# Decode attention over a long K/V cache: TensorE's scores in an inner loop over the two halves of the keys, and the closing steps of a head group ahead of the next group's scores

## The chip, the cores and the metric

The kernel runs on one NeuronCore of a Trainium2 chip. The metric is the device time of one execution in microseconds. A profiled execution gives a trace of every engine: TensorE (PE, with its weight loads as PEld), VectorE (DVE), ScalarE (ACT), GpSimd (POOL) and SyncE (SP, which issues most DMAs). A letter q behind an engine's name is its sequencer, which does the waits, the branches and the register steps. The two matrix memories of the text are SBUF, where tiles lie, and PSUM, where TensorE writes its products.

## The reference

One token for each of two batch rows attends to a cache of 32,768 keys, with 32 query heads in 8 groups of 4 that share a K/V head; a small MLP makes a gate that multiplies the attention's output.

```python
xn = layernorm(x)                        # x: (2, 1, 512)
q = (xn @ wq)                            # 32 heads of 128
scores = q @ k_cache^T * 128 ** -0.5     # k_cache: (2, 8, 32768, 128) bf16, each K/V head for 4 query heads
p = softmax(scores)
s = (p @ v_cache) @ wo                   # wo: (4096, 512)
x1 = xn + hs                             # hs: a gated, time-shifted branch; with one token its shifted parts are zero
g = silu(x1 + gelu(layernorm(x1) @ w3) @ w4)
out = x + s * g
```

The two caches are 268 MB of bf16; the weights that are read are some 12 MB more.

## The kernel before

The work is cut into 16 head groups, one for each batch row and K/V head (`NG = 16`). A group's K is one SBUF tile of 8.4 MB and so is its V. `kbuf` has three half-tiles (slots) and `vbuf` two, so a group's K takes two of the three slots, in turn 0 and 1, then 1 and 2. The keys of a group are treated in two halves (`NPART = 2`), each in 8 rounds (`NR = 8`) of 16 keys on each of 128 partitions.

There is no scheduler: every engine has its own program, written out by hand, with semaphores between them. TensorE and VectorE run a loop over groups (VectorE's body holds two, `par` 0 and 1), ScalarE and GpSimd loop too, and SP's list of DMAs is written out. In a group:

- VectorE transposes K, 16 times 128x1024 int32 (L589), into four buffers `Ts` in turn. Each transpose counts up `t_vt`; from the fifth on each waits until TensorE has used the buffer (`used`).
- TensorE takes the transposes two at a time and makes the scores, four matmuls of 128x512 for each (L698), into the PSUM tile `sc[0]` for the first half and `sc[1]` for the second.
- VectorE takes each half's row maximum (`peak`, L568 and L572), TensorE spreads it (L710), VectorE makes `shift` of it (L600), ScalarE the exponentials (L491), VectorE turns these round into `pt` (L608).
- TensorE multiplies by V into `o` (L722), 32 matmuls for each half, with a `fill` matmul or two ahead of each half that only keep it busy, and then sums the exponentials over the partitions into `S` (L729). ScalarE copies `o` to `ob` (L496) once the products are done.

The **closing steps** of a group turn `o` into its slice of the attention's output. They are `head_oT` on TensorE (L660: eight small fp32 passes over `ob`), `head_on` on VectorE (L543 `den`, L546 `rec`, L547 `recm`, L552 `on`), `head_xp` on TensorE (L666) and `head_out` on VectorE (L559 `xm`, L565 `oXs`), and GpSimd's `put_o` (L513), which copies `oXs` to its place in `oX`. Before, they are done inside the next group's scores: `head_oT` between the two halves on TensorE, `head_on` after the 12th transpose on VectorE (`if i == 1 and r == 3`), `head_xp` after the 13th round on TensorE, `head_out` behind the 16th transpose. The first group does them on values that were set ahead of the loop. After the last group they are done once more, outside of the loops: TensorE goes on in `pe_output` with `head_oT`, L740, a fill, `head_xp`, and then the product with `A_wo`: L760 for five K/V heads, L750 for these summed up (`wsum`, copied by ScalarE in L646), L768 for the other three; VectorE multiplies by the gate and adds x (L647, L648), and two DMAs write the output.

SP's list of loads runs in order on one queue: the weights, K of group 0, V of group 0, then K and V of each group in turn, and last `A_wo` in six parts. Two waits hold it. K of group m waits for `pe.sem`, which TensorE counts up at the last round of the first half of group m-1 (the slot is free then); V of group m waits for `ac.sem`, which ScalarE counts up when the products with V of group m-1 are done, and so does `A_wo` for group 14's. For group 15 alone, K and V come as two DMAs each, a half at a time, with a semaphore for each half.

`t_tv` counts what TensorE has done for VectorE; in a group it counts 20 (`N_T`): the sum, the eight rounds of the first half, oT, the next rounds, xp among them, the rest, and the spread maximum. `used`, `sum_of`, `out_of` and `turned` say at which count a thing is done, and so hold the order of TensorE's program.

Of the kernel before, what the change touches and what calls it, by code (L numbers as in the profile page):

```python
# [8 lines left out]
BF16 = mybir.dt.bfloat16  # L9
# [4 lines left out]
PE = mybir.EngineType.PE  # L14
# [104 lines left out]
def kernel(  # L119
# [51 lines left out]
    def bank(name, cols=512, dt=F32):  # L171
        return psum.tile([128, cols], dt, name=name)
# [54 lines left out]
    oX = sb("oX", [128, 1 + B * Hkv, NQ], BF16)  # L227
    oXz = sb("oXz", [128, Hkv - KC, NQ, OJ - 1 + OM], BF16)

    sc = [bank(f"sc{i}") for i in range(NPART)]  # L230
    o = bank("o")
    S = bank("S")
    oT = bank("oT", rep)
# [66 lines left out]
    def order(m):  # L300
        return (1, 0) if m % 2 == 0 else (0, 1)
# [5 lines left out]
    with tc.tile_critical(sync_engine=mybir.EngineType.Pool, no_gpsimd_drain=True):  # L307
# [153 lines left out]
        for m in range(1, NG):  # L461
            base = m % 2
            if m < NG - 1:
                sp.op(lambda e, m=m, base=base: e.dma_start(
                    out=kbuf[:, base * SLOT:(base + NPART) * SLOT], in_=row_view(A_k_cache, *groups[m])),
                    (pe.sem, pe_0 + m), e_q, inc=(t_k[0], 16))
            else:
                for i, h in enumerate(order(m)):
                    sp.op(lambda e, m=m, h=h, base=base: e.dma_start(
                        out=kbuf[:, (base + h) * SLOT:(base + h + 1) * SLOT],  # L470
                        in_=row_view(A_k_cache, *groups[m])[:, h * SLOT:(h + 1) * SLOT]),
                        (pe.sem, pe_0 + m), inc=(t_k[i], 16))
            load_v(m, (ac.sem, ac_0 + m))
        for i, (a, c, r0, r1) in enumerate(wo_parts):
            cols = slice(r0 * D, r1 * D)
# [52 lines left out]
        N_T = NPART * NR + 4  # L528

        def used(par, n):  # L530
            return t_tv, par * N_T + n + 2 + (n >= NR) + (n >= NR + 5)

        def sum_of(par):
            return t_tv, par * N_T + 1

        def out_of(par, last=False):
            return t_tv, par * N_T + (2 if last else NR + 2)

        def turned(par, last=False):
            return t_tv, par * N_T + (3 if last else NR + 8)  # L540

        def head_on(c, par=0, last=False, behind=None):
            nc.vector.tensor_reduce(  # L543
                out=den[:, :], in_=S[:, 0:NPART * rep].rearrange("p (i h) -> p h i", h=rep),
                axis=AX.X, op=ALU.add).wait_op(*sum_of(par), "sem-ge").then_inc(*c.inc(t_d))
            nc.vector.reciprocal(out=rec[:, :], in_=den[:, :]).wait_op(*c.at(t_d), "sem-ge").then_inc(*c.inc(t_d))  # L546
            nc.vector.tensor_mul(  # L547
                out=recm[:, :, :], in0=rec[:, :].unsqueeze(1).broadcast_to([128, NQ, rep]),
                in1=sel_h[:, :].unsqueeze(2).broadcast_to([128, NQ, rep])).wait_op(*c.at(t_d), "sem-ge").then_inc(*c.inc(t_d))
            e = c.at(t_d)  # L550
            nc.vector.wait_ge(*out_of(par, last))
            ins = nc.vector.tensor_mul(  # L552
                out=on[:, :, :], in0=oT[:, :].unsqueeze(1).broadcast_to([128, NQ, rep]), in1=recm[:, :, :]).wait_op(*e, "sem-ge")
            if last:
                ins.then_inc(t_vt, 1)
                behind()

        def head_out(c, par=0, last=False):
            nc.vector.tensor_mul(  # L559
                out=xm[:, :, :], in0=xp_b[:, :].rearrange("p (r h) -> p r h", r=NQ),  # L560
                in1=mask[:, :].unsqueeze(1).broadcast_to([128, NQ, rep])).wait_op(*turned(par, last), "sem-ge").then_inc(*c.inc(t_d))
            with nc.allow_low_precision(reason="three of the four terms are zero, the fourth is bf16"):
                if last:
                    return ve.op(lambda v: v.tensor_reduce(out=oXz[:, Hkv - KC - 1, :, OJ * B - 1], in_=xm[:, :, :], axis=AX.X, op=ALU.add), c.at(t_d), e_xz0)
                nc.vector.tensor_reduce(out=oXs[:, :], in_=xm[:, :, :], axis=AX.X, op=ALU.add).wait_op(*c.at(t_d), "sem-ge").then_inc(t_vg, 1)  # L565
# [11 lines left out]
        with nc.body("dve_groups", valid_engines=[DVE]):  # L577
            c = Counts()
            for par in range(2):
                nc.vector.wait_ge(*c(t_z))  # L580
                for i, h in enumerate(order(par)):
                    u = par + h
                    kt = kbuf[:, u * SLOT:(u + 1) * SLOT].bitcast(I32)
                    for r in range(NR):
                        n = i * NR + r
                        events = ([c(t_k[i], 16)] if r == 0 else []) + ([used(par, n - T_BUFS)] if n >= T_BUFS else [])
                        for e in events[:-1]:
                            nc.vector.wait_ge(*e)
                        ins = nc.vector.transpose(  # L589
                            out=Ts[n % T_BUFS][:, :].rearrange("p (b t k) -> p t b k", b=NB, t=RT),  # L590
                            in_=kt[:, r * W:(r + 1) * W].rearrange("p (t b k) -> p t b k", b=NB, t=RT))
                        for e in events[-1:]:
                            ins.wait_op(*e, "sem-ge")
                        ins.then_inc(t_vt, 1)
                        if i == 1 and r == 3:
                            peak(c, 0)
                            head_on(c, par)
                head_out(c, par)
                peak(c, 1, *used(par, NT - 1))
                nc.vector.tensor_reduce(  # L600
                    out=shift[:, :], in_=S[:, NPART * rep:NPART * (rep + 32)], axis=AX.X, op=ALU.min).wait_op(t_tv, (par + 1) * N_T, "sem-ge").then_inc(t_shift, 1)
                for h in range(NPART):
                    e = c(t_e)
                    if h == NPART - 1:
                        nc.vector.tensor_mul(
                            out=sm[:, :, :], in0=sel_h[:, :].unsqueeze(1).broadcast_to([128, NPART, rep]),
                            in1=rs[:, :].unsqueeze(2).broadcast_to([128, NPART, rep])).wait_op(*e, "sem-ge").then_inc(t_vg, 1)
                    ins = nc.vector.transpose(  # L608
                        out=pt[h][:, :, :].rearrange("p r (t h) -> p t r h", h=rep),
                        in_=ep[order(par).index(h)][:, :].rearrange("p (t r h) -> p t r h", r=NR, h=rep))  # L610
                    if h < NPART - 1:
                        ins.wait_op(*e, "sem-ge")
                    ins.then_inc(t_vt, 1)
            c(t_tv, 2 * N_T)
            for s_, n in c.totals():
                take(nc.vector, s_, n)
            nc.regs_alu(turn_v, turn_v, 1, op=ALU.add)
            nc.vector.br_lt(turn_v, NG // 2, on_true="dve_groups", on_false="dve_last").branch_hint(hint_v)
        nc.switch_bb("dve_last")

        for b in range(B):
# [4 lines left out]
        e_wd, e_ws, e_s = ((pe.sem, pe.n + NG + i) for i in (1, 2, 3))  # L626


        def own_part():
# [6 lines left out]

        c = Counts()
        e_wide = (ve.sem, ve.n + 2)
        head_on(c, last=True, behind=own_part)
# [41 lines left out]
        pe.n, pe.seen = prologue.n + NG, prologue.seen  # L681
        assert prologue.n == pe_0
        turn = nc.alloc_registers("turn", engines=[PE])
        nc.regs_mov(turn, 0)
# [2 lines left out]
            nc.tensor.wait_ge(s, v)  # L687
        nc.br("pe_groups", engines=[PE])
        with nc.body("pe_groups", valid_engines=[PE]):
            for i in range(NPART):  # L690
                for r in range(NR):
                    if r % 2 == 0:
                        take(nc.tensor, t_vt, 2)
                    Tb = Ts[(i * NR + r) % T_BUFS][:, :].bitcast(BF16).rearrange("p (b c e) -> p b c e", b=NB, e=2)
                    zc = (NR - 1 - r) * rep
                    for nb in range(NB):
                        for w in range(2):
                            ins = nc.tensor.matmul(  # L698
                                sc[i][:, :], lhsT=z[:, nb, w, zc:zc + 128], rhs=Tb[:, nb, :, w],
                                start=(r == 0 and nb == 0 and w == 0),  # L700
                                stop=(r == NR - 1 and nb == NB - 1 and w == 1))
                            if i == 0 and r == NR - 1 and nb == 0 and w == 0:
                                ins.then_inc(pe.sem, 1)
                    ins.then_inc(t_tv, 1)
                    if i == 1 and r == 4:
                        head_xp()
                if i == 0:
                    head_oT()
            take(nc.tensor, t_vt)
            nc.tensor.matmul(  # L710
                S[:, NPART * rep:NPART * (rep + SREP * 32)].rearrange("p (s c) -> p s c", s=SREP), lhsT=same_h[:, :],
# [100 lines left out]
```

## Time and profile before

| | |
|---|---|
| median of 3 runs | 656.33 us (655.88, 656.33, 656.56) |
| profiled execution, first to last instruction (span) | 654.1 us |
| of the median outside of such a span | 2.2 us |
| TensorE busy | 417.4 us (64%) |
| VectorE busy | 379.4 us (58%) |
| ScalarE busy | 39.7 us (6%) |
| bytes moved by DMA | 280.54 MB, 429 GB/s over the span |

The profiled execution's own time is known by its span; the three runs were timed without it. In a line of a timeline the first number is the start in us from the span's start, the second how long the instructions took together, then engine, line, operation, tiles written and read, shapes, and how many were merged (x8); in square brackets stands how long the engine had been idle before and what ended this. In a line on sequencer steps (`PEldq`, `POOLq`) the three numbers are the shortest, the median and the longest in ns. In a line of a table by stretches stand the stretch, its length, busy time and number of instructions of each engine (PE, PEld, DVE, ACT, POOL), TensorE's granted clock as a share of full speed, the DMA engines' share and GB/s.

### The profile page before, as it was taken

To read this page: it belongs to the slowest core of one execution; us is meant where nothing else is said; L and a number is where in the kernel's file an instruction comes from. 1 tells how busy PE (TensorE), PEld (TensorE's weight loads), DVE (VectorE), ACT (ScalarE), POOL (GpSimd) and SP (SyncE) were. 2 spreads that over 40 slices of the span, in tenths; PEclk is the share of its full clock that TensorE was granted. 3 is DMA by queue.
4 is the path that set the end of the run, shared out by engine and by line. 5 is a ranking of instruction groups with operands and counts; after the bars stand their busy time and mean duration, and the time that the engine had idled before them with its cause. 6 is when DMAs were issued, how large, how long until landed. Compare 5 with 4: busy or idle time off the path is not lost. (4 is left out here: it accounts for less than half of the span.)

```text
span 654.1 us, 6304 instructions
## 1 busy us (share of the span) xinstructions
PE 417.4 (64%) x2476; PEld 159.3 (24%) x2476; DVE 379.4 (58%) x541; ACT 39.7 (6%) x90; POOL 10.3 (2%) x44
## 2 busy tenths in 40 slices
PE   1437386574858747485774838667484865748876
PEld 0013132221313212131321313222131322213223
DVE  5348193673919457291854729276481936738772
ACT  1200101000010100001000010100001010000101
POOL 1000000000000000000000000000000000000000
PEclk9859889697997969899796989969698896979999
DMA  8999999999999999998999999999999899999997
GB/s 367 435 449 449 442 393 449 445 449 401 437 445 449 433 405 449 445 449 389 449 445 449 417 421 445 449 445 393 449 445 449 389 449 445 449 425 411 437 429 292
DMA packets 6246, 280.54 MB, mean 429 GB/s; under 512 B 730, under 2 KB 868, under 8 KB 1380
## 3 DMA queue, kind: packets, MB, share of 16 engines
q1 hardware_dynamic: 6232, 280.50, 99.2%
q8 instruction: 2, 0.03, 0.0%
q10 hardware_dynamic: 12, 0.00, 0.0%
HBM read 280.50 MB, written 0.00 MB: 429 GB/s over the span
## 5 line engine op out<-in xcount | busy, mean ns | idle before, releaser
L589 DVE STREAM_TRANSPOSE T<-kbuf 128x1024 int32<-128x1024 int32 x256 | 294.8, 1211 | 180.1 <-DMA kbuf<-in_A_k_cache_dram 173.2
L698 PE MATMUL sc<-T,z 128*128 128x512 bf16 x1024 | 273.1, 420 | 179.5 <-PEq L482 179.2
L698 PEld LDWEIGHTS sc<-T,z 128*128 128x128 bf16 x1024 | 98.9, 104 | 346.6 <-issue 260.2
L722 PE MATMUL o<-vbuf,pt 128*16 128x512 bf16 x1024 | 70.4, 379 | 17.7 <-PEq L482 17.7
L491 ACT ACTIVATE ep<-sc,shift 128x512 bf16<-128x512 f32 x32 | 21.7, 683 | 502.7 <-ACTq L482 502.7
L722 PEld LDWEIGHTS o<-vbuf,pt 128*16 128x16 bf16 x1024 | 27.3, 88 | 64.9 <-issue 42.8
L568 DVE TENSOR_REDUCE mx<-sc 128x1 f32<-128x512 f32 x32 | 21.5, 672 | 30.1 <-PE sc L698 30.1
L673 PE MATMUL pro<-ob,comb 128*2 128x512 f32 x66 | 33.7, 592 | 0.0
L608 DVE STREAM_TRANSPOSE pt<-ep 128x512 bf16<-128x512 bf16 x32 | 22.6, 708 | 15.0 <-ACT ep L491 15.0
L710 PE MATMUL S<-mxr,same_h 128*128 128x448 f32 x32 | 15.8, 576 | 18.4 <-PEq L482 18.4
L660 PEld LDWEIGHTS oT<-sel_o,ob 128*128 128x128 f32 x136 | 17.7, 191 | 3.4 <-issue 0.7
L729 PE MATMUL S<-sm,ones_f 128*128 128x448 f32 x32 | 16.3, 592 | 0.0
L660 PE MATMUL oT<-sel_o,ob 128*128 128x4 f32 x136 | 16.2, 242 | 0.0
L600 DVE TENSOR_REDUCE shift<-S 128x1 f32<-128x64 f32 x16 | 3.6, 225 | 18.8 <-PE S L710 18.8
L496 ACT COPY ob<-o 128x512 f32<-128x512 f32 x16 | 9.4, 587 | 78.6 <-ACTq L482 78.6
L513 POOL COPY oX<-oXs 128x4 bf16 (+1 forms) x16 | 3.0, 188 | 518.7 <-POOLq L482 518.7
L710 PEld LDWEIGHTS S<-mxr,same_h 128*128 128x128 f32 x32 | 4.8, 188 | 26.1 <-issue 26.1
L572 DVE TENSOR_SCALAR mxr<-row_of,mx 128x32 f32<-128x32 f32 x32 | 7.7, 241 | 1.1
L673 PEld LDWEIGHTS pro<-ob,comb 128*2 128x2 f32 x66 | 4.2, 83 | 14.0 <-issue 10.4
L393 PE MATMUL qrb<-ident,xs_bf 34*128 34x34 bf16 x4 | 0.3, 198 | 11.1 <-DVE xs_bf L356 11.1
L729 PEld LDWEIGHTS S<-sm,ones_f 128*128 128x128 f32 x32 | 4.8, 188 | 6.9 <-issue 6.9
L506 POOL TENSOR_TENSOR z<-qr,quad 128x64 bf16<-128x64 bf16 x16 | 4.7, 294 | 103.2 <-POOLq L482 87.7
(100 smaller groups left out, 78.5 us busy)
## 6 DMA issues: line engine op xcount, KB each, us to landing
kbuf<-in_A_k_cache_dram SPq DMA_DIRECT2D x2, 4096.0 KB, 22.4
vbuf<-in_A_v_cache_dram SPq DMA_DIRECT2D x2, 4096.0 KB, 21.7
kbuf<-in_A_wq_dram SPq DMA_DIRECT2D x1, 4096.0 KB, 12.4
vbuf<-in_B_w_dram SPq DMA_DIRECT2D x2, 1792.0 KB, 18.0
kbuf<-in_A_wo_dram SPq DMA_DIRECT2D x1, 2048.0 KB, 30.8
kbuf<-in_A_wo_dram SPq DMA_DIRECT2D x3, 512.0 KB, 31.9
kbuf<-in_A_wo_dram SPq DMA_DIRECT2D x1, 384.0 KB
kbuf<-in_A_k_cache_dram SPq DMA_DIRECT2D x15, 27.5
```

The lines of the kernel that those rows point to most:

```text
L491: nc.scalar.activation(out=ep[i][:, :], in_=sc[i][:, :], func=ACT.Exp, scale=inv_sqrt_dh, bias=shift[:, :], accum_out=rs[:, i:i + 1]).then ...
L496: nc.scalar.copy(out=ob[:, :], in_=o[:, :]).then_inc(t_ob, 1)
L568: ins = nc.vector.tensor_reduce(out=mx[:, i:i + 1], in_=sc[i][:, :], axis=AX.X, op=ALU.max)
L572: ins = nc.vector.tensor_scalar_mul(out=mxr[:, i, :], in0=row_of[:, :], scalar1=mx[:, i:i + 1]).wait_op(*c.at(t_d), "sem-ge")
L589: ins = nc.vector.transpose(out=Ts[n % T_BUFS][:, :].rearrange("p (b t k) -> p t b k", b=NB, t=RT), in_=kt[:, r * W:(r + 1) * W].rearrange ...
L608: ins = nc.vector.transpose(out=pt[h][:, :, :].rearrange("p r (t h) -> p t r h", h=rep), in_=ep[order(par).index(h)][:, :].rearrange("p (t ...
L660: ins = nc.tensor.matmul(oT[:, :], lhsT=ob[:, t * Dh:(t + 1) * Dh], rhs=sel_o[:, t, :], start=(t == 0), stop=(t == VT - 1))
L673: nc.tensor.matmul(pro[0:B, :], lhsT=comb[:, 0:B], rhs=ob[:, :], start=True, stop=True)
L698: ins = nc.tensor.matmul(sc[i][:, :], lhsT=z[:, nb, w, zc:zc + 128], rhs=Tb[:, nb, :, w], start=(r == 0 and nb == 0 and w == 0), stop=(r = ...
L710: nc.tensor.matmul(S[:, NPART * rep:NPART * (rep + SREP * 32)].rearrange("p (s c) -> p s c", s=SREP), lhsT=same_h[:, :], rhs=mxr[:, :, :]. ...
L722: ins = nc.tensor.matmul(o[32 * j:32 * j + VT * rep, :], lhsT=pt[h][:, r, a * VT * rep:(a + 1) * VT * rep], rhs=vt[:, u * VT:(u + 1) * VT, ...
L729: nc.tensor.matmul(S[:, 0:SSUM * NPART * rep].rearrange("p (s c) -> p s c", s=SSUM), lhsT=ones_f[:, :], rhs=sm[:, :, :].rearrange("p i h - ...
```

## The change

TensorE's body of a group now begins with `head_oT`, a wait for VectorE's `on`, and `head_xp`; only then come the scores. These are a loop of the machine over the two halves (`nc.Fori`), whose body holds 8 rounds, 32 matmuls; before, all 16 rounds were written out. The two score tiles become one tile of two banks, `sc2`, and the matmuls write to a column that comes from the loop's register. TensorE counts up `pe.sem` in each half, so twice a group, and the waits of K's loads are renumbered to the same event as before.

VectorE's body of a group now begins with `head_on`, the wait for GpSimd's `z`, and `head_out`; then come all 16 transposes, with the first half's maximum behind the 12th as before. `on` counts up `t_vt`, for TensorE to wait on. The counts in `used`, `out_of` and `turned` follow. The end of the kernel keeps its order.

```diff
@@ buffers
-    sc = [bank(f"sc{i}") for i in range(NPART)]
+    sc2 = bank("sc", 512 * NPART)
+    sc = [sc2[:, 512 * i:512 * (i + 1)] for i in range(NPART)]
@@ the loads of K
-                    (pe.sem, pe_0 + m), e_q, inc=(t_k[0], 16))
+                    (pe.sem, pe_0 + NPART * (m - 1) + 1), e_q, inc=(t_k[0], 16))
...
@@ counts
         def used(par, n):
-            return t_tv, par * N_T + n + 2 + (n >= NR) + (n >= NR + 5)
+            return t_tv, par * N_T + n + 4
...
-        def out_of(par, last=False):
-            return t_tv, par * N_T + (2 if last else NR + 2)
-
-        def turned(par, last=False):
-            return t_tv, par * N_T + (3 if last else NR + 8)
+        def out_of(par):
+            return t_tv, par * N_T + 2
+
+        def turned(par):
+            return t_tv, par * N_T + 3
...
@@ head_on
-            if last:
-                ins.then_inc(t_vt, 1)
+            ins.then_inc(t_vt, 1)
+            if behind:
                 behind()
...
@@ VectorE's body of a group
             for par in range(2):
+                head_on(c, par)
                 nc.vector.wait_ge(*c(t_z))
+                head_out(c, par)
                 for i, h in enumerate(order(par)):
...
                         if i == 1 and r == 3:
                             peak(c, 0)
-                            head_on(c, par)
-                head_out(c, par)
                 peak(c, 1, *used(par, NT - 1))
...
@@ TensorE's body of a group
-            for i in range(NPART):
+            head_oT()
+            take(nc.tensor, t_vt)
+            head_xp()
+            with nc.Fori(0, NPART, engines=[PE]) as i:
                 for r in range(NR):
                     if r % 2 == 0:
                         take(nc.tensor, t_vt, 2)
-                    Tb = Ts[(i * NR + r) % T_BUFS][:, :].bitcast(BF16).rearrange("p (b c e) -> p b c e", b=NB, e=2)
+                    Tb = Ts[r % T_BUFS][:, :].bitcast(BF16).rearrange("p (b c e) -> p b c e", b=NB, e=2)
...
-                                sc[i][:, :], lhsT=z[:, nb, w, zc:zc + 128], rhs=Tb[:, nb, :, w],
+                                sc2[:, bass.ds(i * 512, 512)], lhsT=z[:, nb, w, zc:zc + 128], rhs=Tb[:, nb, :, w],
...
-                            if i == 0 and r == NR - 1 and nb == 0 and w == 0:
+                            if r == NR - 1 and nb == 0 and w == 0:
                                 ins.then_inc(pe.sem, 1)
                     ins.then_inc(t_tv, 1)
-                    if i == 1 and r == 4:
-                        head_xp()
-                if i == 0:
-                    head_oT()
```

More of the change, by code (lines that the diff above doesn't have):

```diff
@@ L471 @@
                         in_=row_view(A_k_cache, *groups[m])[:, h * SLOT:(h + 1) * SLOT]),
-                        (pe.sem, pe_0 + m), inc=(t_k[i], 16))
+                        (pe.sem, pe_0 + NPART * (m - 1) + 1), inc=(t_k[i], 16))
             load_v(m, (ac.sem, ac_0 + m))
@@ L530, in used, with head_on @@
         def used(par, n):
-            return t_tv, par * N_T + n + 2 + (n >= NR) + (n >= NR + 5)
+            return t_tv, par * N_T + n + 4
         def sum_of(par):
             return t_tv, par * N_T + 1
-        def out_of(par, last=False):
-            return t_tv, par * N_T + (2 if last else NR + 2)
-        def turned(par, last=False):
-            return t_tv, par * N_T + (3 if last else NR + 8)
-        def head_on(c, par=0, last=False, behind=None):
+        def out_of(par):
+            return t_tv, par * N_T + 2
+        def turned(par):
+            return t_tv, par * N_T + 3
+        def head_on(c, par=0, behind=None):
             nc.vector.tensor_reduce(
@@ L550, in head_on @@
             e = c.at(t_d)
-            nc.vector.wait_ge(*out_of(par, last))
+            nc.vector.wait_ge(*out_of(par))
             ins = nc.vector.tensor_mul(
                 out=on[:, :, :], in0=oT[:, :].unsqueeze(1).broadcast_to([128, NQ, rep]), in1=recm[:, :, :]).wait_op(*e, "sem-ge")
-            if last:
-                ins.then_inc(t_vt, 1)
+            ins.then_inc(t_vt, 1)
+            if behind:
                 behind()
@@ L560, in head_out @@
                 out=xm[:, :, :], in0=xp_b[:, :].rearrange("p (r h) -> p r h", r=NQ),
-                in1=mask[:, :].unsqueeze(1).broadcast_to([128, NQ, rep])).wait_op(*turned(par, last), "sem-ge").then_inc(*c.inc(t_d))
+                in1=mask[:, :].unsqueeze(1).broadcast_to([128, NQ, rep])).wait_op(*turned(par), "sem-ge").then_inc(*c.inc(t_d))
             with nc.allow_low_precision(reason="three of the four terms are zero, the fourth is bf16"):
@@ L625 @@
                 in1=sel_h[:, :].unsqueeze(1).unsqueeze(3).broadcast_to([128, KW, rep, NQ])), e_oX[m + KW - 1])
-        e_wd, e_ws, e_s = ((pe.sem, pe.n + NG + i) for i in (1, 2, 3))
+        e_wd, e_ws, e_s = ((pe.sem, pe.n + NPART * NG + i) for i in (1, 2, 3))
         def own_part():
@@ L638 @@
         e_wide = (ve.sem, ve.n + 2)
-        head_on(c, last=True, behind=own_part)
+        head_on(c, behind=own_part)
         e_oX[NG - 1] = head_out(c, last=True)
@@ L680 @@
         prologue, pe = pe, Queue(nc.tensor, pe.sem)
-        pe.n, pe.seen = prologue.n + NG, prologue.seen
+        pe.n, pe.seen = prologue.n + NPART * NG, prologue.seen
         assert prologue.n == pe_0
```

## The prediction

> **What bounds the kernel now.** I read the page first: its span and its DMA queue.
>
> ```profile
> span 654.1 us, 6304 instructions
> q1 hardware_dynamic: 6232, 280.50, 99.2%
> ```
>
> One queue carries all 280.50 MB, and its packets fill 99.2% of the span. So the kernel is a stream of K and V loads with everything else laid beside it, and a change to the compute can matter in two ways only: if it makes a load start too late to keep the queue full, or if it makes the work behind the last loads end later than they land. For the first I read the timeline of a group in the middle (SPq rows are DMA issues, L448 a V load, L464 a K load).
>
> ```profile
> 304.54 1.02 PE L729 MATMUL S<-sm,ones_f 128*128 128x448 f32 x2
> 304.78 0.33 SPq L448 DMA_DIRECT2D vbuf<-in_A_v_cache_dram  x1
> 312.62 5.75 DVE L589 STREAM_TRANSPOSE T<-kbuf 128x1024 int32<-128x1024 int32 x5 [11.89 <-DMA kbuf<-in_A_k_cache_dram]
> 324.21 0.33 SPq L464 DMA_DIRECT2D kbuf<-in_A_k_cache_dram  x1
> ```
>
> VectorE waited 11.89 us for K. The V load behind that K was issued at 304.78, 7.8 us before the K landed, so the queue never ran dry. The closing sum of the group before (L729) began at 304.54: VectorE and TensorE have 8.08 us in which nothing else can start, because the next group's K is not there. For the second way I read the chain of waits and the last groups.
>
> ```profile
> 617.12 33.53 DMA kbuf<-in_A_wo_dram
> ```
>
> The chain that ended last is the load of `A_wo`, the last load of all; L768, L647 and L648 follow it. Here is how groups 14 and 15 lie before it.
>
> ```profile
> 583.11 5.75 DVE L589 STREAM_TRANSPOSE T<-kbuf 128x1024 int32<-128x1024 int32 x5 [10.97 <-DMA kbuf<-in_A_k_cache_dram]
> ...
> 598.10 0.16 DVE L543 TENSOR_REDUCE den<-S 128x4 f32<-128x8 f32 x1
> ...
> 598.80 4.61 DVE L589 STREAM_TRANSPOSE T<-kbuf 128x1024 int32<-128x1024 int32 x4
> ...
> 612.08 9.13 DVE L589 STREAM_TRANSPOSE T<-kbuf 128x1024 int32<-128x1024 int32 x8 [1.76 <-DMA kbuf<-in_A_k_cache_dram]
> ...
> 614.12 1.02 PE L729 MATMUL S<-sm,ones_f 128*128 128x448 f32 x2
> ...
> 621.88 4.62 DVE L589 STREAM_TRANSPOSE T<-kbuf 128x1024 int32<-128x1024 int32 x4 [0.67 <-DMA kbuf<-in_A_k_cache_dram]
> ...
> 627.97 4.61 DVE L589 STREAM_TRANSPOSE T<-kbuf 128x1024 int32<-128x1024 int32 x4
> ...
> 643.29 1.02 PE L729 MATMUL S<-sm,ones_f 128*128 128x448 f32 x2
> ```
>
> Group 15 is unlike the others: its K comes in two halves, and the first is there at 612.08, before group 14 is done on TensorE (L729 at 614.12). Today VectorE starts on it at once. This is the one place where the kernel uses the overlap that the change gives up.
>
> **The closing steps in the middle groups: nothing.** Their chain is head_oT (TensorE), `on` (VectorE), head_xp (TensorE), `xm` and `oXs` (VectorE). The kernel runs the same chain at its end, where nothing hides it:
>
> ```profile
> 644.31 1.02 PE L660 MATMUL oT<-sel_o,ob 128*128 128x4 f32 x8
> 645.45 0.17 DVE L552 TENSOR_TENSOR on<-oT,recm 128x16 bf16<-128x16 f32 x1 [0.52 <-PE oT L660]
> 646.30 0.18 PE L666 MATMUL xp<-on,sel_w 128*128 128x16 bf16 x1
> 646.52 0.17 DVE L559 TENSOR_TENSOR xm<-xp,mask 128x16 f32<-128x16 f32 x1 [0.28 <-PE xp L666]
> 646.73 0.18 DVE L564 TENSOR_REDUCE oXz<-xm 128x4 bf16<-128x16 f32 x1
> ```
>
> From the start of L729 at 643.29: oT starts 1.02 later, and `on` ends at 645.62, 2.33 after. At the end of the kernel head_xp stands behind other work; without it TensorE would take up `on` as it takes up `mxr` in the next two rows, 0.14 after its end (606.53 to 606.67).
>
> ```profile
> 606.29 0.24 DVE L572 TENSOR_SCALAR mxr<-row_of,mx 128x32 f32<-128x32 f32 x1
> 606.67 0.99 PE L710 MATMUL S<-mxr,same_h 128*128 128x448 f32 x2 [1.15 <-PEq L482]
> ```
>
> Then 0.22 from xp to `xm` and 0.21 to the reduction, whose successor on VectorE starts about 0.1 later: 2.33 + 0.14 + 0.22 + 0.21 + 0.1 = 3.0 us from L729 to the first transpose that VectorE may now do. In a middle group K lands 8.08 after L729, so 5.1 us are to spare, and the closing chain costs nothing there. What queues behind the new waits is, on VectorE, all 16 transposes of the next group, and on TensorE its scores; on SP, the next K load waits for the first half's last round (the new count names the same event: one increment for each half, and NPART*(m-1)+1 is the first of group m-1), so its issue stays where it is. GpSimd's put_o follows `oXs` and comes earlier; put_z keeps its place.
>
> **Inside a group: 0.70 us saved.** `den`, `rec`, `recm` and `on` stood between the 12th and the 13th transpose, from 598.10 to 598.80. They go, and the rest of the group moves up by 0.70. `xm` and `oXs` stood where VectorE waits for TensorE's last scores anyway: nothing. In the middle groups the 0.70 only lengthens the wait for K. oT (0.95 us on TensorE) leaves the boundary between the halves, where VectorE sets the pace: nothing.
>
> **The inner loop.** It adds a backward branch between the halves, and an output address from a register. The nearest rows are the outer loop's branch on TensorE and the register step that GpSimd makes for an address that depends on its loop:
>
> ```profile
> L734 PEldq COMPARE_BRANCH  x16: 76/208/228, 70.6 to 641.8; - x16
> L506 POOLq FUSED_REGOPS  x15: 55/55/55, 67.7 to 609.8; - x15
> ```
>
> The branch is 0.21 us. It takes the place of 0.95 us of oT, on an engine that waits for transposes in the second half. For the register step the ends are: nothing (one step for a pass, or steps beside running matmuls), and 0.055 us on each of 32 matmuls, unhidden. A gain is excluded, because VectorE paces the half. I take nothing: matmuls are queued ahead of the array, and 0.055 fits into the 0.245 of each (the row under the rivals). The upper end is a rival below.
>
> **Group 15: where the time comes from.** All of this goes by the profiled execution. Group 14 starts at 583.11 as before, since K sets it, and is 0.70 shorter: L729 at 613.42. VectorE starts group 15 at 613.42 + 3.0 = 616.42, 4.34 later than the 612.08 of today. Both halves of K are there by 621.88, and the 9th transpose, eight spacings of 1.14 (13.74 for 12, below) after 616.42, comes at 625.5, so it waits for no K. How long it then takes to the 13th transpose is read from whole groups: 583.11 to 598.80 is 15.69 in group 14, and the longest and the shortest of groups 0 to 14 are these two:
>
> ```profile
> 158.14 5.75 DVE L589 STREAM_TRANSPOSE T<-kbuf 128x1024 int32<-128x1024 int32 x5 [11.47 <-DMA kbuf<-in_A_k_cache_dram]
> ...
> 174.43 1.24 DVE L589 STREAM_TRANSPOSE T<-kbuf 128x1024 int32<-128x1024 int32 x1
> 274.01 13.74 DVE L589 STREAM_TRANSPOSE T<-kbuf 128x1024 int32<-128x1024 int32 x12 [11.55 <-DMA kbuf<-in_A_k_cache_dram]
> ...
> 289.22 2.36 DVE L589 STREAM_TRANSPOSE T<-kbuf 128x1024 int32<-128x1024 int32 x2
> ```
>
> That is 16.29 and 15.21. What differs is how long TensorE's clock stays at half. I take group 14's 15.69, less 0.70: 14.99. The 13th transpose then starts at 616.42 + 14.99 = 631.41, against 627.97: 3.44 later. From there to L729 it is 15.32 in both groups (598.80 to 614.12, 627.97 to 643.29), so nothing in that stretch waits for a load, and L729 comes at 643.29 + 3.44 = 646.73.
>
> The clock bears on this. In the middle groups it is at half when scores start:
>
> ```profile
> 310.00:312.00 2.00, 0.00 (x0) 0.00 (x0) 0.00 (x0) 0.00 (x0) 0.00 (x0) 0.50 1.14 492
> ```
>
> This is 4.4 to 6.4 us after TensorE's last work (305.56). [...]
>
> **How much the end can hide.** These rows are the stretch behind L729 at the end.
>
> ```profile
> 646.41 1.04 PE L760 MATMUL qrb<-kbuf,T 128*2 128x512 bf16 x16
> 647.29 0.39 PE L760 MATMUL qrb<-kbuf,oX 128*2 128x512 bf16 x4
> 648.62 0.61 PE L768 MATMUL pro<-kbuf,oXz 128*4 128x128 bf16 x16 [0.94 <-DMA kbuf<-in_A_wo_dram]
> 649.07 0.81 PE L750 MATMUL pro<-T,comb 128*4 128x128 f32 x8
> 649.74 0.43 PEld L768 LDWEIGHTS pro<-kbuf,oXz 128*4 128x4 bf16 x16 [0.15 <-DMA kbuf<-in_A_wo_dram]
> 650.69 0.62 PE L768 MATMUL pro<-kbuf,oXz 128*4 128x128 bf16 x16 [0.33 <-DMA kbuf<-in_A_wo_dram]
> 647.74 0.59 ACT L646 COPY T<-qrb 128x512 f32<-128x512 f32 x1 [3.57 <-PE qrb L760]
> 651.35 0.28 DVE L647 TENSOR_TENSOR sg<-pro,g 36x128 f32<-36x128 f32 x1 [4.29 <-PE pro L768]
> ```
>
> Now 8.06 us from L729 (643.29) to `sg` (651.35), with waits for A_wo inside. Without them: L760 runs on to 647.29 (its second group starts before the first has ended, so no wait); the copy of `wsum` ends at 648.33, and L768's first 16 fit beside it; L750 at about 648.43, the next 16 of L768 0.65 later at 649.08 (649.07 to 649.74, less the wait), the last 16 another 0.43 on at 649.51, and `sg` 0.66 after that (650.69 to 651.35): 650.17. This is 6.88 us, so 1.2 us of the delay is hidden by the load. `sg` comes at 646.73 + 6.88 = 653.61, against 651.35: 2.26 later.
>
> **Sum.** 3.44 - 1.18 = 2.3 us, with 1.8 and 2.9 at the two ends of the row of groups. The span is 654.1; the runs shown are 655.88, 656.33 and 656.56, 2.2 above it at the median. The delay is added to that: 656.33 + 2.3 = 658.6, own range 657.7 to 659.6 with 0.3 for the spread of runs.
>
> **The rivals.** First, TensorE becomes the pace in the scores. At full clock 8 score matmuls take
>
> ```profile
> 632.73 1.96 PE L698 MATMUL sc<-T,z 128*128 128x512 bf16 x8 [0.26 <-PEq L482]
> ```
>
> 0.245 each. With 0.055 unhidden on each, four take 1.20, over the 1.145 of a transpose (13.74 for 12 above): 0.055 in each of 16 rounds, and 0.44 in the last two rounds that VectorE waits for, 1.3 us a group. It counts in groups 14 and 15 alone: 2.6 us more, 661.2. It decides from 0.04 us a matmul on. For it: no row shows TensorE with a register address. Against it: GpSimd's step is taken once for an instruction, and here 32 share one address. 0.13.
>
> Second, not slower: the load of A_wo still ends last and hides all. That holds while group 15 is late by under 1.2 us, and gives 656.3 to 656.9. For it: today's chain ends in that load. Against it: the 13th transpose would have to come 12.7 us after 616.42, and 12 transposes alone take 13.74; only loads that land 2 us later relative to group 14's K would do it, and the three runs lie within 0.7. 0.10.
>
> Third, the queue runs dry: if the loop added more than the 5.1 us to spare in each group, every microsecond over it would be paid in 15 groups, 671 for one. Nothing in the rows comes near: 0.03. That it gets faster has no row for it, as the queue is full: 0.02.
>
> **How the numbers follow.** The forecast has 0.72. About 0.2% (1.3 us) is what a measurement here can tell from no change. Same: the second rival and 0.04 from the forecast's low edge, 0.14. Slower: the rest of the forecast, the first and third rivals, 0.84. The range takes the forecast's own and reaches to the first rival above and half way to the second below: 656.9 to 661.4.
>
> **What would show it.** In the changed profile: the middle groups' transposes still wait for K; the closing chain lies 1 to 3 us behind L729; the 13th transpose comes 15.0 after the first; group 15's first transpose starts 3.0 behind L729 of group 14, not on a K landing; the last L768 shows no wait for A_wo, and the chain that ended last runs back through L729 and the transposes of group 15. It is wrong if that chain still ends in the A_wo load, if score matmuls are spaced over 0.285, or if issues on SP come after the K before them has landed.

## The result and the profile after

The change takes 658.87 us (657.43 to 659.56 in 8 runs), against 656.29 before, also in 8 runs. One of the 8 before took 1381.36 us, for a reason that nothing here shows, and is left out of the ratio; the other seven lie between 655.88 and 656.56. The ratio is 1.0038, with a 95% interval from 1.0029 to 1.0048: slower by 2.6 us, where 2.3 was forecast. The profiled execution spans 656.8 us, 2.7 more than that of before. Line numbers move by a few after the edit: K's transposes are L592, the scores L702, `den` L544, `oXs` L566, oT L661, xp L667, `sg` L648; L729, L760 and L768 keep theirs.

The page's head and queue, and the waits of VectorE (engine, line, for whom, us in total, times, longest):

```profile
span 656.8 us, 6464 instructions
q1 hardware_dynamic: 6232, 280.50, 98.8%
DVE den L544 <- PE S L729: 77.4, 16, 4.9
DVE T L592 <- DMA kbuf<-in_A_k_cache_dram: 74.6, 15, 6.5
```

Before, the second of these waits was:

```profile
DVE T L589 <- DMA kbuf<-in_A_k_cache_dram: 173.2, 17, 12.7
```

VectorE's wait for K fell from 173.2 us in 17 waits to 74.6 in 15, and 77.4 us of wait for the group before came in. Read by itself this looks like a large shift; it is one idle stretch cut in two by the closing steps, which now lie inside it. The queue still fills 98.8% of the span. The chain of waits has changed its kind. These are steps of it, from the last closing sum to the gate:

```profile
647.52 0.95 PE S L729 x2
...
650.63 1.18 PE qrb L760 x20
...
653.11 0.91 PE pro L768 x32
...
654.05 0.29 DVE sg L648
```

No load is in the chain any more; before, 33.5 us of it were the load of `A_wo`. Groups 14 and 15 in the timeline:

```profile
578.48 0.17 DVE L566 TENSOR_REDUCE oXs<-xm 128x4 bf16<-128x16 f32 x1
583.47 5.83 DVE L592 STREAM_TRANSPOSE T<-kbuf 128x1024 int32<-128x1024 int32 x5 [4.83 <-DMA kbuf<-in_A_k_cache_dram]
586.14 9.23 PE L702 MATMUL sc<-T,z 128*128 128x512 bf16 x32 [7.91 <-PEq L483]
...
597.70 0.65 DVE L569 TENSOR_REDUCE mx<-sc 128x1 f32<-128x512 f32 x1
598.53 4.62 DVE L592 STREAM_TRANSPOSE T<-kbuf 128x1024 int32<-128x1024 int32 x4
...
613.86 1.02 PE L729 MATMUL S<-sm,ones_f 128*128 128x448 f32 x2
...
616.75 0.17 DVE L566 TENSOR_REDUCE oXs<-xm 128x4 bf16<-128x16 f32 x1
616.84 5.82 DVE L592 STREAM_TRANSPOSE T<-kbuf 128x1024 int32<-128x1024 int32 x5
...
632.12 4.62 DVE L592 STREAM_TRANSPOSE T<-kbuf 128x1024 int32<-128x1024 int32 x4
634.63 1.96 PE L702 MATMUL sc<-T,z 128*128 128x512 bf16 x8 [1.16 <-PEq L483]
...
647.45 1.02 PE L729 MATMUL S<-sm,ones_f 128*128 128x448 f32 x2
```

And two rows of group 14 in the kernel before, its first scores and the maximum of its first half:

```profile
585.62 9.32 PE L698 MATMUL sc<-T,z 128*128 128x512 bf16 x32 [8.66 <-PEq L482]
...
597.26 0.65 DVE L568 TENSOR_REDUCE mx<-sc 128x1 f32<-128x512 f32 x1
```

Group 14 still waits 4.83 us for K after its closing steps are done. Group 15 starts at 616.84, straight behind `oXs` and with no wait in brackets: its K had been there. In the kernel before, it started at 612.08. The 4.76 us of delay become 4.15 at the 13th transpose (632.12 against 627.97) and 4.16 at L729, since the 12 transposes and the maximum took 15.28 where before group 15 took 15.89 with `head_on` and a wait for K's second half inside. Part of the 4.16 costs nothing, since the kernel before waits behind L729 for the load of `A_wo`. The same stretch in the change:

```profile
650.56 1.04 PE L760 MATMUL qrb<-kbuf,T 128*2 128x512 bf16 x16
651.43 0.39 PE L760 MATMUL qrb<-kbuf,oX 128*2 128x512 bf16 x4
651.64 0.61 PE L768 MATMUL pro<-kbuf,oXz 128*4 128x128 bf16 x16
...
652.51 0.61 PE L750 MATMUL pro<-T,comb 128*4 128x128 f32 x8
652.94 1.06 PE L768 MATMUL pro<-kbuf,oXz 128*4 128x128 bf16 x32
```

From 647.45 to `sg` at 654.05 are 6.60 us, with no wait for `A_wo`; before they were 8.06 with such waits. So 1.46 us are hidden, and 4.16 - 1.46 = 2.70 is what `sg` comes later (654.05 against 651.35), the whole of the difference between the two spans. Of the 2.70, 0.36 came in ahead of both groups: K of group 14 landed that much later in this execution (583.47 against 583.11).

### The profile page after: what moved, and what is told of

Same layout as the page of the kernel before. It is cut to its first block, busy times and chain, and to the rows that moved or that the text cites. A ratio compares the mean times of both kernels' runs of the same rounds, so it can differ in the third digit from the quotient of the medians.

```text
span 656.8 us, 6464 instructions
## 1 busy us (share of the span) xinstructions
PE 435.1 (66%) x2476; PEld 162.9 (25%) x2476; DVE 384.3 (59%) x541; ACT 39.7 (6%) x90; POOL 10.3 (2%) x44
## 3 DMA queue, kind: packets, MB, share of 16 engines
q1 hardware_dynamic: 6232, 280.50, 98.8%
## 5 line engine op out<-in xcount | busy, mean ns | idle before, releaser
L702 PE MATMUL sc<-T,z 128*128 128x512 bf16 x1024 | 278.5, 426 | 155.4 <-PEq L483 153.1
L592 DVE STREAM_TRANSPOSE T<-kbuf 128x1024 int32<-128x1024 int32 x256 | 296.6, 1215 | 84.7 <-DMA kbuf<-in_A_k_cache_dram 74.6
L702 PEld LDWEIGHTS sc<-T,z 128*128 128x128 bf16 x1024 | 99.8, 104 | 327.5 <-issue 240.8
L544 DVE TENSOR_REDUCE den<-S 128x4 f32<-128x8 f32 x17 | 2.8, 165 | 77.4 <-PE S L729 77.4
L661 PEld LDWEIGHTS oT<-sel_o,ob 128*128 128x128 f32 x136 | 17.3, 199 | 15.6 <-issue 15.6
L661 PE MATMUL oT<-sel_o,ob 128*128 128x4 f32 x136 | 18.3, 258 | 3.6 <-PEq L483 3.6
L729 PE MATMUL S<-sm,ones_f 128*128 128x448 f32 x32 | 16.3, 592 | 0.0
L553 DVE TENSOR_TENSOR on<-oT,recm 128x16 bf16<-128x16 f32 x17 | 3.0, 175 | 10.0 <-PE oT L661 10.0
L440 PE MATMUL sc<-vbuf,h_bf 128*2 128x512 bf16 x14 | 6.1, 624 | 2.4 <-DVE h_bf L437 2.4
```

What stands on the lines that cost most here:

```text
L592: ins = nc.vector.transpose(out=Ts[n % T_BUFS][:, :].rearrange("p (b t k) -> p t b k", b=NB, t=RT), in_=kt[:, r * W:(r + 1) * W].rearrange ...
L661: ins = nc.tensor.matmul(oT[:, :], lhsT=ob[:, t * Dh:(t + 1) * Dh], rhs=sel_o[:, t, :], start=(t == 0), stop=(t == VT - 1))
L702: ins = nc.tensor.matmul(sc2[:, bass.ds(i * 512, 512)], lhsT=z[:, nb, w, zc:zc + 128], rhs=Tb[:, nb, :, w], start=(r == 0 and nb == 0 and ...
L729: nc.tensor.matmul(S[:, 0:SSUM * NPART * rep].rearrange("p (s c) -> p s c", s=SSUM), lhsT=ones_f[:, :], rhs=sm[:, :, :].rearrange("p i h - ...
```

## The experiments

Theory A is that of the prediction: VectorE starts group 15 late, and nothing else costs. Theory B is that the inner loop costs, by its branch or by the column from a register. Each time stands beside that of the kernel before on the same chip, and each ratio is to that.

### The two parts of the change alone

**Closing steps ahead, scores written out.**

```diff
-            with nc.Fori(0, NPART, engines=[PE]) as i:
+            for i in range(NPART):
...
-                                sc2[:, bass.ds(i * 512, 512)], lhsT=z[:, nb, w, zc:zc + 128], rhs=Tb[:, nb, :, w],
+                                sc[i][:, :], lhsT=z[:, nb, w, zc:zc + 128], rhs=Tb[:, nb, :, w],
```

> The closing steps ahead of the scores as in the change, but all 16 rounds of scores written out, with no inner loop and no column from a register. Theory A (the cost is the late start of group 15 alone, and the inner loop costs nothing): 658.6 to 659.0 us, as the change; first transpose of group 15 3.0 us behind the closing sum of group 14; the step from the first to the second half's scores falls from 0.82 to about 0.25 us and nothing else gets shorter by it. Rival B (the inner loop's branch and register column are what costs): 656.3 us, as before.

**Inner loop, closing steps inside the scores** (here against the change; the counts in `used` and `turned` follow). TensorE does oT ahead of its loop and xp behind it, so the order is not quite that of the kernel before; what matters is that VectorE may again start a group as soon as K lands.

```diff
@@ VectorE's body of a group
-                head_on(c, par)
                 nc.vector.wait_ge(*c(t_z))
-                head_out(c, par)
...
                             peak(c, 0)
+                            head_on(c, par)
                 peak(c, 1, *used(par, NT - 1))
+                head_out(c, par)
@@ TensorE's body of a group
             head_oT()
-            take(nc.tensor, t_vt)
-            head_xp()
             with nc.Fori(0, NPART, engines=[PE]) as i:
...
+            head_xp()
             take(nc.tensor, t_vt)
```

> The inner loop over the halves as in the change, but the closing steps back inside the scores: head_oT ahead of TensorE's loop, head_on behind VectorE's 12th transpose, head_xp behind TensorE's loop, head_out behind the second half's maximum. VectorE can again start group 15 when its first half of K lands. Theory A: 656.3 us within 0.5, as before, the load of A_wo ends the kernel again. Rival B: 658.9 us, as the change.

**The change again.**

> The change itself, on the same chip as the others of this call: 658.9 us by both theories. Its profile gives a second look at the same sum: group 15's first transpose 3.0 us behind the closing sum of group 14, 15.33 us from the 13th transpose to the last closing sum, and 15.0 to 15.8 between first and 13th transpose, by the phase of TensorE's clock.

Measured, against 656.10 us before on this chip: without the loop 658.16 us, ratio 1.0036 (1.0022 to 1.0049); with the loop and the closing steps inside 655.98, ratio 0.9999 (0.9990 to 1.0008); the change 659.00, ratio 1.0038 (1.0024 to 1.0052). The first two runs say the same from two sides: the order is what costs, and the loop by itself costs nothing that shows. Without the loop 658.16 lies below the 658.6 that A had named, while its interval covers the change's ratio; whether the loop adds some tenths of a microsecond once the order has put it on the path of the end, the times don't settle, but two profiles further down do. In the timeline of the run with the loop and the old order, group 15 starts when its K lands, and the last line is from its chain of waits:

```profile
612.37 4.62 DVE L590 STREAM_TRANSPOSE T<-kbuf 128x1024 int32<-128x1024 int32 x4 [1.68 <-DMA kbuf<-in_A_k_cache_dram]
```

```profile
617.48 33.45 DMA kbuf<-in_A_wo_dram
```

`A_wo` ends the kernel again. What the loop itself adds is seen in the sequencer steps of the change (ns: shortest, median, longest):

```profile
L702 PEldq FUSED_REGOPS  x32: 46/46/46, 43.4 to 629.3; - x32
L694 PEldq COMPARE_BRANCH  x32: 76/144/225, 51.0 to 637.0; - x32
```

There are 32 register steps, one for each half of each of 16 groups, not one for each of 1024 matmuls. Eight score matmuls still take 1.96 us (634.63 above). Only the start moves: in the run without the loop the first score comes 2.50 us after the first transpose (the first two of the next rows), in the change 2.67 (583.47 to 586.14) and 2.51 before (583.11 to 585.62). The x40 says that the scores of the two halves run on there without a break.

```profile
617.13 5.74 DVE L592 STREAM_TRANSPOSE T<-kbuf 128x1024 int32<-128x1024 int32 x5
619.63 12.05 PE L702 MATMUL sc<-T,z 128*128 128x512 bf16 x40 [2.84 <-PEq L483]
...
632.59 1.24 DVE L592 STREAM_TRANSPOSE T<-kbuf 128x1024 int32<-128x1024 int32 x1
```

The second profile of the change, from the same chip, has these rows:

```profile
617.11 5.82 DVE L592 STREAM_TRANSPOSE T<-kbuf 128x1024 int32<-128x1024 int32 x5
...
632.74 2.36 DVE L592 STREAM_TRANSPOSE T<-kbuf 128x1024 int32<-128x1024 int32 x2
```

In these two profiles TensorE's clock is back at full speed in the same half microsecond (591.0 to 591.5 in group 14, 625.0 to 625.5 in group 15), so they can be compared. From the first to the 13th transpose of group 15 it is 15.46 us without the loop and 15.63 with it, and 15.47 (583.35 to 598.82) and 15.64 (583.16 to 598.80) in group 14. So in this pair the loop costs 0.17 us in each of the two groups, 0.3 us of the change's 2.6 to 2.9. In the run with the loop and the old order the chain ends in the load of `A_wo`, and the time is no longer than before.

### When group 15 starts

If the start of group 15 sets the end, a later start must cost more, whatever the order. Both kernels were run with the K of the last group as one DMA.

```diff
-        nc.gpsimd.sem_inc(t_k[1], 16 * (NG - 1))
+        nc.gpsimd.sem_inc(t_k[1], 16 * NG)
...
             base = m % 2
-            if m < NG - 1:
+            if m < NG:
```

> The kernel before, with K of the last group as one DMA in place of two halves, so that group 15 cannot start on TensorE's or VectorE's side before all of its K has landed (621.9 in the trace of before). Theory A (the end is set by when VectorE starts group 15): first transpose at 621.9, 13th 15.7 later at 637.6, 9.6 later than before, of which the load of A_wo hides 1.2 to 1.5: 656.3 + 8.2 = 664.5 us. Rival C (the last loads set the end, and compute at the end has room): 656.3 to 657.

> The change, with K of the last group as one DMA. Now the closing steps have their room in group 15 too, since the K lands 5 us behind them. Theory A: the same start as the run with the kernel before, less the 0.70 us that head_on takes inside the group: 663.8 us, and so faster than that run by 0.5 to 0.9. Rival B (the loop or the order costs time of its own): slower than that run by 2 to 3 us.

Measured, against 655.93 before: the kernel before with K whole 663.87 us, ratio 1.0123 (1.0108 to 1.0139); the change with K whole 663.84, ratio 1.0118 (1.0103 to 1.0134). The first is 0.6 below the 664.5 that A had named. Rival C is out: the loads are the same bytes in the same order, and the end moved by 7.9 us. Rival B, which asked for 2 to 3 us, is out: with the same start the change is not slower. The starts are in the timelines, first the kernel before, then the change:

```profile
621.72 5.75 DVE L589 STREAM_TRANSPOSE T<-kbuf 128x1024 int32<-128x1024 int32 x5 [11.09 <-DMA kbuf<-in_A_k_cache_dram]
627.85 8.00 DVE L589 STREAM_TRANSPOSE T<-kbuf 128x1024 int32<-128x1024 int32 x7 [0.38 <-PE sc L698]
635.78 0.65 DVE L568 TENSOR_REDUCE mx<-sc 128x1 f32<-128x512 f32 x1
...
637.32 4.61 DVE L589 STREAM_TRANSPOSE T<-kbuf 128x1024 int32<-128x1024 int32 x4
```

```profile
621.75 5.83 DVE L592 STREAM_TRANSPOSE T<-kbuf 128x1024 int32<-128x1024 int32 x5 [5.34 <-DMA kbuf<-in_A_k_cache_dram]
628.04 1.25 DVE L592 STREAM_TRANSPOSE T<-kbuf 128x1024 int32<-128x1024 int32 x1 [0.46 <-PE sc L702]
629.75 6.88 DVE L592 STREAM_TRANSPOSE T<-kbuf 128x1024 int32<-128x1024 int32 x6 [0.46 <-PE sc L702]
636.55 0.65 DVE L569 TENSOR_REDUCE mx<-sc 128x1 f32<-128x512 f32 x1
...
637.39 4.62 DVE L592 STREAM_TRANSPOSE T<-kbuf 128x1024 int32<-128x1024 int32 x4
```

Three starts of group 15 (612.1, 616.8 and 621.7) go with 656, 658.9 and 663.9 us. From the second to the third, where nothing is hidden any more, 4.9 us of start make 5.0 us of time.

What A had expected between these two runs, 0.5 to 0.9 us in favour of the change, did not show. The rows say where it went in this pair. `head_on` is gone: from the maximum to the 13th transpose it is 0.84 us against 1.54, the 0.70 saved. But the first 12 transposes took 14.80 against 14.06, as VectorE waited twice for TensorE and not once. Two things lie behind this in the traces. By stretches of half a microsecond the granted clock is at half until about 627.9 in the kernel before and until about 629.9 in the change; and with the loop the sixth transpose comes 6.29 us after the first, not 6.13. With four runs each, a gain of a few tenths in the time is neither shown nor excluded.

### TensorE's clock at the start of group 15

```diff
             head_xp()
+            fill(6)
             with nc.Fori(0, NPART, engines=[PE]) as i:
```

> The change with six fill matmuls (about 0.5 us each) behind head_xp, which keep TensorE busy until the scores of group 15 start; in the middle groups some 4 us without work remain. Theory A with its clock term: TensorE is at full speed when group 15's scores start, VectorE waits for no buffer, the 13th transpose comes 14.5 us after the first where the change has 15.28, and the time falls by 0.7 to 0.9 us on average, to 658.0 to 658.2, with less spread among runs. Rival (the clock at the start does not matter, VectorE sets the pace): 15.3 and 658.9 us.

Measured: 658.71 us against 656.10 before, ratio 1.0044 (1.0030 to 1.0058), no gain. The edit was mis-sized, and the timeline shows it:

```profile
615.95 5.31 PE L674 MATMUL pro<-ob,comb 128*2 128x512 f32 x12
621.20 4.02 PE L703 MATMUL sc<-T,z 128*128 128x512 bf16 x17
```

Six fills are 12 passes and 5.31 us, and the scores had to wait for them. So it was run with three.

> The change with three fills behind head_xp. The run with six showed that a fill takes 0.88 us, not 0.5, so that six held TensorE's scores of group 15 back by 2.2 us. Three end at about 618.6, just before the scores of group 15 can start. Theory A with its clock term: full speed from the first score of group 15, no wait of VectorE for a buffer, 14.4 us from the first to the 13th transpose (15.3 and 15.6 in the two profiles of the change), 658.0 to 658.3 us. Rival (the clock does not matter): 658.9.

Measured: 658.07 us (657.19 to 658.65 in 7 runs), ratio 1.0029 (1.0018 to 1.0040), against 655.96 before. Two stretches of a table by stretches (the granted clock stands ahead of the last two numbers), the first from the change, the second from this run, and then this run's timeline:

```profile
620.00:622.00 2.00, 2.00 (x6) 0.62 (x5) 2.00 (x3) 0.00 (x0) 0.00 (x0) 0.50 1.22 524
```

```profile
620.00:622.00 2.00, 1.45 (x7) 0.69 (x8) 2.00 (x3) 0.00 (x0) 0.00 (x0) 1.00 0.91 393
```

```profile
617.66 13.62 DVE L592 STREAM_TRANSPOSE T<-kbuf 128x1024 int32<-128x1024 int32 x12
...
632.05 1.24 DVE L592 STREAM_TRANSPOSE T<-kbuf 128x1024 int32<-128x1024 int32 x1
```

At full clock (1.00 in all four stretches from 616 to 624) the 12 transposes run through without a wait, and it is 14.39 us from the first to the 13th, as expected, where the change, at 0.50 in the stretch above, has 15.28. That the clock sets this stretch is shown in the trace. A gain in time is not: against the kernel before on its own chip this run is 2.1 us slower, where the change was 2.6 and 2.9, and the intervals overlap. In its profiled execution, the longest of the seven, K of group 14 landed at 584.09, 0.62 later than in that of the change, so group 15 started 0.82 later (617.66), its 13th transpose came 0.07 earlier, and both spans are 656.8.

### How much the load of A_wo hides

A delay of known length was put on the closing chain of the kernel before, on VectorE behind `on` (two and six memsets). Line numbers move by two in these runs: L762 is the L760 of before, L770 the L768.

```diff
         def own_part():
+            for j in range(6):
+                nc.vector.memset(kbuf.bitcast(F32)[:, SLOT // 2 + 512 * j:SLOT // 2 + 512 * (j + 1)], 0.0)
```

> The kernel before, with two memsets of 128x512 f32 (0.54 us each) on VectorE behind `on` of the last closing, ahead of the product that TensorE's first matmuls with A_wo wait for: 1.1 us on the closing chain at the end. Theory A (the load of A_wo hides 1.2 by the prediction, 1.46 by the trace of the change): 656.3 us, no change. Rival (nothing hides there): 657.4.

> The kernel before, with six such memsets in the same place: 3.24 us on the closing chain at the end. Theory A: 3.24 less 1.2 to 1.46, so 658.1 to 658.3 us, and the chain that ended last no longer ends in the load of A_wo. Rival (nothing hides there): 659.5.

Measured: with two 655.99 us, ratio 1.0001 (0.9992 to 1.0010), against 655.93 before. The profile has them at 1.03 us, and `sg` where it was (651.34 against 651.35):

```profile
645.67 1.03 DVE L631 MEMSET kbuf<- 128x512 f32 x2
...
651.34 0.28 DVE L649 TENSOR_TENSOR sg<-pro,g 36x128 f32<-36x128 f32 x1 [3.64 <-PE pro L770]
```

So at least 1.0 us is hidden. With six: 659.38, ratio 1.0049 (1.0035 to 1.0063): 3.4 us, all of the delay and more, as the rival had it. Here the timeline of the end:

```profile
645.47 3.19 DVE L631 MEMSET kbuf<- 128x512 f32 x6
649.35 1.88 PE L762 MATMUL qrb<-kbuf,T 128*2 128x512 bf16 x16 [3.09 <-DVE T L636]
654.90 0.28 DVE L649 TENSOR_TENSOR sg<-pro,g 36x128 f32<-36x128 f32 x1 [5.24 <-PE pro L770]
```

The 16 matmuls behind the memsets took 1.88 us and not 1.04: TensorE had been idle for 3.09 us and ran at half its clock (the granted clock is 0.50 from 647.5 to 654.0). So the rival's number came out by another way, and one more run had to tell them apart, with three more fills ahead of head_xp at the end (`fill(4)` for `fill(1)`), so that TensorE stays busy beside the memsets.

> The run with six memsets on the closing chain at the end, and four fills in place of one ahead of head_xp there, so that TensorE is not left idle for 3.1 us behind the memsets. In the run without them its first matmuls with A_wo took 1.88 us for 16, twice the 1.04 of before, so its 3.4 us contain a slower clock. Theory A (the load of A_wo hides 1.46): the memsets delay by 3.03, so 656.0 + 3.03 - 1.46 = 657.6 us, and those 16 take 1.04 again. Rival (nothing hides, the memsets cost their full length): 659.0 to 659.4.

Measured: 657.58 us, ratio 1.0025 (1.0015 to 1.0035), against 655.96 before.

```profile
643.08 1.02 PE L731 MATMUL S<-sm,ones_f 128*128 128x448 f32 x2
649.35 1.04 PE L762 MATMUL qrb<-kbuf,T 128*2 128x512 bf16 x16 [0.51 <-DVE T L636]
652.83 0.28 DVE L649 TENSOR_TENSOR sg<-pro,g 36x128 f32<-36x128 f32 x1 [3.18 <-PE pro L770]
```

With the 16 back at 1.04, the run costs 1.6 us. How much is hidden follows from the rows: from the last closing sum to `sg` it is now 9.75 us (643.08 to 652.83), against 6.60 in the change, where nothing waits for `A_wo`, and 8.06 in the kernel before. So the memsets delay by 3.15 us, a little more than the 3.03 that was expected, and cost 1.69: 1.46 us are hidden, as in the change's own trace.

No version came out that beats both kernels. The one with the loop and the closing steps inside equals the kernel before, and there the queue is full and the last load ends the work.

## Why the prediction was right

The mechanism and the sign were as forecast, and the size nearly: 658.87 against 658.6, well inside 656.9 to 661.4. By its steps, in the profiled execution:

- **Middle groups, nothing.** Right. `oXs` is done at 578.65, K lands 4.83 us later by the wait; 5.1 were said to be to spare.
- **3.0 us from L729 to the first transpose.** 2.98 (613.86 to 616.84).
- **0.70 saved inside a group.** 0.71 from the maximum to the 13th transpose (597.70 to 598.53, against 597.26 to 598.80 before). But not all of it reached the 13th transpose, by the next point: that came 15.06 after the first, where 15.69 less 0.70 is 14.99.
- **The inner loop, nothing.** Not quite. The rival with a register step on each matmul is out, as there is one for a half. What the prediction did not price is the start: the first score comes 0.16 later. While the clock is at half, VectorE waits for the buffers that these scores release (0.46 us ahead of the sixth transpose of group 15, at 623.12), so this is passed on: 0.17 us a group in the pair of profiles above, in the two groups that count.
- **14.99 us from the first to the 13th transpose of group 15.** 15.28, inside the ends of its row of groups (16.29 and 15.21, less 0.70). In the second profile of the change it was 15.63 (617.11 to 632.74), a little over the upper of these, 15.59.
- **15.32 from there to L729.** 15.33.
- **6.88 from L729 to `sg`.** 6.60: the hidden part was put at 1.2 and is 1.46. Of the 0.28, 0.22 is one step, from L750 to the second 16 of L768: the prediction took 0.65, though its own rows less their wait give 0.52 (0.67 - 0.15), and it is 0.43 (652.51 to 652.94).

The misses of 0.29 in group 15 and of 0.28 at the end have opposite signs and nearly cancel, which is luck. What is left between the 2.26 of the sum and the 2.70 of the profile is K of group 14, which landed 0.36 later than in the profile of before, and 0.08 from group 14 itself. The landing is no part of the sum, and whether the change has a part in it is open: it came at 583.16 in the second profile of the change.

The rival "the load hides all" was right in its mechanism: it does hide 1.0 us in full, as the two memsets show, and by the 1.46 it would have decided if group 15 had been late by less than that.

## What to carry to other kernels

A kernel whose DMA queue is 99% full can still be slowed by a reordering (2.6 us here), and the place to look is the last pass, where, as here, no wait for a load is left between two groups: ask there what started early before and what it now waits for, and take off what the last load still hides. In the middle of such a kernel large shifts in the waits (here 77 us from one cause to another) may cost nothing. A step that is free while something hides it, such as the loop here, has its price once another change puts it on the path (0.17 us in each of two groups). A delay put on one engine as a probe can change another's clock (six memsets on VectorE left TensorE at 0.50), so keep that engine busy while probing.

## What the runs showed of the hardware that I had not expected

A pause of 3.09 us on TensorE in the run with six memsets was enough to halve its clock for the work behind it (16 matmuls in 1.88 us and not 1.04). By stretches of half a microsecond, the granted clock fell at about 647.2, 0.9 us after TensorE's last matmul (xp, done at 646.26), and was back at about 654.0. In the kernel before, it fell 2.6 us after the last matmul of group 13 (576.96 to 579.52) and 4.3 us after that of group 6 (305.56 to 309.87), and it stayed at 1.00 through a gap of 1.86 us in group 14 (up to 601.31). So the length of a gap alone does not tell; what sets the moment of the fall, no run here shows. The stretches at half clock, worked out from the same half microseconds, come in few lengths: about 3.4 us ahead of group 14's scores with six fills (586.3 to 589.7), 6.8 in the run with six memsets and in group 15 of the change (617.1 to 623.9), 10.2 in group 14 of the kernel before (579.52 to 589.76), 13.7 in group 3 of the change (152.89 to 166.55). In each of the profiles of before and of the change, from 65 us on, any two changes of the clock lie a whole multiple of 3.4133 us apart, to within 0.02 (28 and 30 changes; the length is fitted to them).

In the change the oT and xp matmuls between L729 and the scores of group 15 did not keep the clock up: it fell at about 617.1, 0.6 us after xp, and stood at 0.50 in the stretch from 620 to 622.

The change's runs spread over 2.1 us (657.43 to 659.56), where eleven runs with the loop and the old order spread over 0.8 (655.77 to 656.55). In the five profiles with the closing steps ahead and K in halves (the change twice, without the loop, with six and with three fills), the stretches outside of the first 12 transposes are alike within 0.02 us. What differs is when K of group 14 lands (583.16 to 584.09), and the time from the first to the 13th transpose (14.83 to 15.64 in group 14, 14.39 to 15.85 in group 15). That the clock, at half for a time that differs, makes the spread is therefore likely and not shown: the landing has its part, and the seven runs with three fills, whose profile has full clock in group 15, still spread over 1.5 us.

The loop on TensorE costs little where TensorE has slack: 0.046 us for the register column, once for a half, at most 0.23 for the branch, and 0.16 by which the first score of a group comes later; with the loop and the old order the time is 655.98 us, against 656.10 before.
